# A SwiGLU and attention kernel: from slots with planned steps to one string of single-engine steps, with one ring for the three-pass blocks

## The chip, the cores and the metric

The kernel runs on one core of a Trainium2 chip. The metric is the time on the device in microseconds. Before the change it is 1538.06 us, the median of three runs (1537.92 to 1538.15). The profile is of one more execution.

The engines are TensorE (PE, with its weight loads as PEld), VectorE (DVE), ScalarE (ACT), GpSimd (POOL) and SyncE (SP), which here only issues transfers. Matrix products land in PSUM, of which the kernel uses eight banks of 128 rows by 512 fp32 numbers (five `gv`, two `acc`, one `u3`); all else lies in SBUF.

## The reference

There are four batches of 12416 rows with 128 channels. An attention with 32 inducing points squeezes each batch to 32 rows `h`, and a second one spreads `h` back over all rows. Its output goes through an RMS norm and a SwiGLU block of width 1536.

```python
def mab(q, kv):
    s = scale * (q @ kv.transpose(0, 2, 1))
    a = np.exp(s - s.max(-1, keepdims=True))
    a /= a.sum(-1, keepdims=True) + 1e-09
    return a @ kv
h = mab(I, x)                       # I: the inducing points, once per batch
x = mab(x, h).reshape(B * S, D)     # 49664 x 128

rms = np.sqrt(np.mean(x * x, axis=-1, keepdims=True) + 1e-06)
xn = x / rms * rms_g
g = xn @ w_gate                     # 128 -> 1536
val = xn @ w_val
return (g / (1 + np.exp(-g)) * val) @ w_out
```

## The kernel before

**Units and blocks.** Each batch is cut into 25 units of columns: 20 of 512, four of 480 and one of 256. The width of 1536 is cut into 12 slices `j`. A block is one slice of one unit, so there are 4 x 25 x 12 = 1200 blocks. The second attention isn't computed as such: its output is a mix of the 32 rows of `h`, so `h` is multiplied into the gate and value weights beforehand (`stack`, tiles `sg` and `sv`), and a unit enters as its attention weights, split into a high and a low half and stacked (`seam`, `gather`, tile `a`).

**One block** is made in `slot`: the gate matmul (L743), silu on ACT (L751), the value matmul (L754), and their product on DVE (L760), the factor. Gates and values share five PSUM banks (`gv`). A gate's bank is free after silu. A value's bank is free after the product, if the product goes to an SBUF tile `u`, or later, if the product stays in the bank.

**The third product**, factor times `w_out`, is summed over the 12 blocks of a unit in the bank `acc`. It has two forms. A plain block multiplies in fp32 (L676, `acc<-u,wo`). A three-pass block is split into parts that each take one pass: `hi` times one weight and `lo` times another are summed in the bank `u3` (L700, L702), and their difference `d` times a third goes to `acc` (L676). There are 819 three-pass blocks and 381 plain ones. Of the 819, 619 are "sums": the factor stays in its PSUM bank, ACT makes a scaled `hi` from it (L725) and DVE makes `lo` from `hi` and the bank (L726). The other 200 are "differences": the factor goes to SBUF, ACT makes the high half (L729), POOL makes `lo` (L730), and ACT scales the high half down (L734). In both, POOL then makes `d` in a tile of its own (L735), and afterwards all three matmuls are issued one after the other in `project3`.

**Tiles.** Three-pass blocks take sets of three SBUF tiles: four sets in old tiles of `xn`, and two more that lie in the spare `sg` and `sv` tiles and are lent for part of each batch (`lend`). Factors in SBUF take nine tiles `u0` to `u8`.

**Order.** Every engine runs its instructions in the order in which they were written. The order is made by a loop over slots. Attention and seam steps are set into slots by the lists `places`; inside a slot, the string `ordered` says where third products are issued; a split begins one slot after its product (`soon`), the difference one slot after that. A step such as `scores2` (L440) or `stack` contains the instructions of several engines. Where exponentials of the attention are near, silu is replaced by tanh, one more DVE pass (L748) and a scaled product (L757), so that ACT needn't change its table: 14 blocks.

**Other lines named below.** L448 subtracts the row maximum from the scores, both operands in SBUF: on POOL, but on DVE for the first set of a batch. L350 multiplies the maxima by a mask on DVE, both in SBUF. L279 and L287 belong to the set-up, which decodes the weights. L543 scales the attention weights on POOL, in place. L341, L390, L469, L483 and L523 are matmuls of the attention and the seams.

```python
hi, lo, d = (one[:, 0:T] for one in kws["sets"][where])
...
nc.scalar.activation(hi, v, AF.Copy, scale=(1.0 - 2.0 ** -13) * 2.0 ** -12)
nc.vector.scalar_tensor_tensor(out=lo, in0=hi.bitcast(F32), scalar=-4096.0, in1=v,
                               op0=ALU.mult, op1=ALU.add)
...
nc.gpsimd.tensor_tensor(out=d, in0=hi.bitcast(F32), in1=lo.bitcast(F32), op=ALU.subtract)
```

Of the kernel before, what the change touches and what calls it, by code (L numbers as in the profile page):

```python
# [18 lines left out]
P = 128  # L19
R = 4  # L20
# [3 lines left out]
def kernel(  # L24
# [75 lines left out]
    RING, RESERVE, HELD, SILU = 4, 7, 9, 3  # L100
    LENT = (RING, RING + 1)
# [41 lines left out]
    def load_channels(b, s, k):  # L143

        w = R * per[s]
        if not k:
            xT[b, s] = xtp.tile([P, w * m], F32, name=f"xT{s}")
        nc.sync.dma_start(out=xT[b, s][ts(k, m), :].rearrange("p (w c) -> p w c", c=m),
                          in_=xrows[ds(b * N + start[s], P * per[s]), ts(k, m)].rearrange("(i w) c -> i w c", i=m))
# [159 lines left out]
    def attention(b, load_next):  # L309
# [34 lines left out]
        def scores1(s):  # L344
            nc.vector.tensor_scalar(out=sc[b][:, cols1[s]], in0=scores(s, indT[:], R, per[s]), scalar1=1.0, scalar2=None,
                                    op0=ALU.mult, op1=ALU.max, accum_out=st["gmx"][:, s:s + 1])
# [31 lines left out]
        def sum_h(*sets):  # L378
# [12 lines left out]
            if b and sets[0]:  # L391
                nc.vector.tensor_tensor(out=hl[:, 0:C], in0=hl[:, 0:C], in1=ps[:, 0:C], op=ALU.add)
            elif b:
                nc.scalar.copy(out=hl[:, 0:C], in_=ps[:, 0:C])

        def fold_l():

            nc.vector.reduce_sum(out=st["hl"][:, C:C + 1], in_=st["ls"][:, 0:st["n"]], axis=AX.X)
            ps = bank()
            nc.tensor.matmul(ps[:, 0:1], fold[:].rearrange("p q m -> p (q m)"), st["hl"][:, C:C + 1], start=True, stop=True)  # L400
            rl = st["rl"] = small.tile([P, 1], F32, name="rl")
            nc.vector.reciprocal(out=rl[:], in_=ps[:, 0:1])
# [8 lines left out]
        def turn_h():  # L411

            ps = bank()
            nc.tensor.matmul(ps[:, 0:P], st["hn"], fold[:].rearrange("p q m -> p (q m)"), start=True, stop=True)
            hT = st["hT"] = once.tile([P, P], F32, name="hT")
            if b:
                nc.scalar.copy(out=hT[:], in_=ps[:, 0:P])
                hg = st["hg"] = once.tile([P, P], F32, name="hg")
                nc.scalar.activation(hg[:], ps[:, 0:P], AF.Copy, scale=gam)
            else:  # L420
                nc.vector.tensor_copy(out=hT[:], in_=ps[:, 0:P])
# [5 lines left out]
        def square_h():  # L427
# [4 lines left out]
            ps = bank()  # L432
            nc.tensor.matmul(ps[:, 0:m], st["hT"][:], st["hT"][:, 0:m], start=True, stop=True)
            for q in range(R):
                to, of_ = gram[b][ts(q, m), ts(q, m)], ps[ts(q, m), 0:m]
                nc.scalar.activation(to, of_, AF.Copy, bias=1e-6, scale=1.0 / C)

        def scores2(s):
            ps = scores(s, st["hT"][:, 0:m], quarters[s], per2[s])
            nc.vector.transpose(out=sc[b][rows2[s], cols2[s]], in_=ps)  # L440

        def row_max(s):
            mx = st["mx2"] = small.tile([P, 16], F32, name="mx2")[rows2[s], 0:per2[s]]
            nc.vector.reduce_max(out=mx, in_=weights(b, s), axis=AX.X)

        def sub_max(s):
            n, v, mx = per2[s], weights(b, s), st["mx2"]
# [16 lines left out]
        def stack(i):  # L464


            ps = bank()
            for c, w in enumerate(st.pop(("w", i))):
                nc.tensor.matmul(ps[ts(c, m), :], st["hg"][:, 0:m], w, start=True, stop=True)  # L469
            hi, lo = st["halves", i] = [worker([P, 512], F32R, n) for n in ("whi", "wlo")]  # L470
            rows = slice(0, NC * m)
            nc.scalar.copy(out=hi[rows, :], in_=ps[rows, :])
            nc.vector.tensor_tensor(out=lo[rows, :], in0=ps[rows, :], in1=hi[rows, :].bitcast(F32), op=ALU.subtract)
# [33 lines left out]
    def seam(b, s):  # L507
# [41 lines left out]
        def split():  # L549
# [4 lines left out]
            else:  # L554
                nc.vector.tensor_copy(out=hi[rows, 0:w], in_=aT[rows, 0:w])
            engine.tensor_tensor(out=lo[rows, 0:w], in0=aT[rows, 0:w], in1=hi[rows, 0:w].bitcast(F32), op=ALU.subtract)

        return [turn_a, square, times, scale, root, apply, turn_b, split]
# [11 lines left out]
    plain, kara, waiting = [], [], []  # L570

    def soon(k, step):

        waiting.append([k, step])

    def wait():

        for one in waiting:
            one[0] -= 1
        while any(not one[0] for one in waiting):  # L580
            one = next(one for one in waiting if not one[0])
            waiting.remove(one)
            one[1]()

    def give(group):

        for kind in group:
            (plain if kind == "p" else kara).pop(0)()

    def split_wo(step):  # L590

        if not step:
            kws["first"] = xnp.tile([P, half + NK, C], F32R, name=f"xn{full - 1}")
            rings = [xnp.tile([P, RING, 512], F32R, name=f"xn{full - 4 + n}") for n in range(3)]
            kws["sets"] = [[ring[:, n, :] for ring in rings] for n in range(RING)]
            idle.extend(range(RING))
# [10 lines left out]
        for g in range(2):  # L607
# [8 lines left out]
            if at == 4:  # L616
                nc.gpsimd.tensor_tensor(out=part(2, g)[0], in0=part(1, g)[1], in1=part(0, g)[1], op=ALU.subtract)
            if at == 6:
                scaled(0, g, 4096.0)

    idle, leaving = [], []

    def lend(b, k, idle, leaving):

        if k == (20 if not b else 2):
            idle += LENT
            return True
        if b + 1 < B and k == 184:
            leaving += [n for n in LENT if n not in idle]
            idle[:] = [n for n in idle if n not in LENT]  # L630
        assert k != 192 or not leaving

    def give_back(n, idle, leaving):

        leaving.remove(n) if n in leaving else idle.append(n)

    def lend_tiles():

        tiles = [stk.tile([P, F], F32R, name=name) for name in ("sg", "sv")]
        kws["sets"][RING:] = [[t[:, ts(n, 512)] for n in range(3)] for t in tiles]  # L640

    def split_last(step):

        n = NJ - NK
        if not step:
            kws["last"] = xtp.tile([P, 3 * n, C], F32R, name="xT0")
        one, (whi, wlo, ws) = wo[:, NK:NJ, :], (kws["last"][:, ts(kind, n), :] for kind in range(3))
        if step == 0:
            nc.scalar.activation(whi, one, AF.Copy, scale=1.0 - 2.0 ** -13)
            nc.gpsimd.tensor_tensor(out=wlo, in0=one, in1=whi.bitcast(F32), op=ALU.subtract)  # L650
        if step == 1:
            nc.scalar.activation(wlo, wlo.bitcast(F32), AF.Copy, scale=4096.0)
            nc.gpsimd.tensor_tensor(out=ws, in0=wlo.bitcast(F32), in1=whi.bitcast(F32), op=ALU.subtract)
        if step == 2:
            nc.scalar.activation(whi, whi.bitcast(F32), AF.Copy, scale=4096.0)

    def weight_of(kind, j):
        if j >= NK:
            return kws["last"][:, kind * (NJ - NK) + j - NK, :]
# [3 lines left out]
    def ffn(b, u):  # L663

        s, q = units[u]
        T = per2[s] * m
        a = moving.pop((b, u))
        sg, sv = stacks[b]
        acc = ps_acc.tile([P, 512], F32, name="acc")
        nk = sum((b, u, j) in kinds for j in range(NJ))  # L670
        st = {"left": NJ, "k": nk}
        if nk:
            st["o"] = None

        def project(lhsT, rhs, to):
            nc.tensor.matmul(to, lhsT, rhs, start=st["left"] == NJ, stop=st["left"] == 1)  # L676
            st["left"] -= 1
            if not st["left"]:
                soon(1, finish)

        def finish():
            o = st["o"] if nk else outp.tile([P, 512], F32, name="o")
            whole = o[:, 0:T].rearrange("p (q n) -> p q n", q=R)
            if nk:
                nc.vector.tensor_tensor(out=whole, in0=in_order(acc[:, 0:T]), in1=whole, op=ALU.add)
            else:
                nc.vector.tensor_copy(out=whole, in_=in_order(acc[:, 0:T]))

            def turn():
                nc.vector.transpose(out=o[:, 0:T], in_=o[:, 0:T])  # L690
                soon(2, lambda: store(o))

            soon(1, turn)

        def project3(j, where):
            if st["k"] == nk:
                st["u"] = ps_u.tile([P, 512], F32, name="u3")
            ups = st["u"]
            hi, lo, d = (one[:, 0:T] for one in kws["sets"][where])
            nc.tensor.matmul(ups[:, 0:T], weight_of(0, j), halves_in_turn(hi), start=st["k"] == nk, stop=False)  # L700
            st["k"] -= 1
            nc.tensor.matmul(ups[:, 0:T], weight_of(1, j), halves_in_turn(lo), start=False, stop=not st["k"])  # L702
            if not st["k"]:
                o = st["o"] = outp.tile([P, 512], F32, name="o")
                nc.scalar.activation(o[:, 0:T].rearrange("p (q n) -> p q n", q=R), in_order(ups[:, 0:T]), AF.Copy,  # L705
                                     scale=1.0 + 2.0 ** -12)
# [609 lines left out]
```

## Time and profile before

| | us |
|---|---|
| median of three runs | 1538.06 |
| time of the profiled execution | 1538.19 |
| span of the profiled execution, first to last instruction | 1536.4 |
| POOL differences, L735, 128 x 512: mean of one | 1.285 |
| POOL low halves, L730, 128 x 512: mean of one | 1.290 |
| DVE low halves, L726, 128 x 512: mean of one | 0.677 |
| DVE products, L760, 128 x 512: mean of one, to SBUF / in PSUM | 0.674 / 0.686 |
| ACT silu, L751, 128 x 512: mean of one | 0.600 |
| start of the first gate matmul / of the last | 47.5 / 1528.4 |

The page gives busy times by engine, the chain of waits that ended last, and groups of instructions by line. The stretch view gives busy times by engine between two moments. The timeline gives single instructions with start and length. On DVE, ACT and POOL the length of an instruction reaches a little into the next one when they follow closely: DVE instructions of 512 columns that take 0.68 start 0.60 apart, POOL's of 1.285 start 1.24 apart. All gates lie between 47.5 and 1528.4 us; before that the weights are decoded and the first batch's attention runs.

### The profile page before, as it was taken

What the parts mean: (1) busy time and instruction counts of PE and PEld (TensorE: products, weight loads), DVE (VectorE), ACT (ScalarE), POOL (GpSimd) and SP (SyncE); (2) the same over time, 40 slices, a digit from 0 to 9 for tenths busy, and PEclk for the clock granted to TensorE, in tenths of its full rate; (3) what the DMA queues carried; (4) which work ended last, traced back from release to release, by engine and by line L of the source; (5) the groups of instructions that cost most, each with busy time, mean ns of one, the idle gap of its engine ahead of it and who ended that gap; (6) DMA issues with size and microseconds to landing.
All of it is one profiled execution on the core that took longest, in us unless ns stands there. A gap on an engine that the chain in (4) does not pass through costs nothing.

```text
span 1536.4 us, 26105 instructions
## 1 busy us (share of the span) xinstructions
PE 1518.3 (99%) x7141; PEld 1091.8 (71%) x7141; DVE 1442.3 (94%) x2519; ACT 1292.2 (84%) x2501; POOL 1418.5 (92%) x1158
## 2 busy tenths in 40 slices
PE   8999999999999999999999999999999999999998
PEld 6556667767776667776777667676677777777776
DVE  6999999999999998999999999899999999999997
ACT  5777889888888889887988888978798888888886
POOL 1379999999999999999999999899989999999997
PEclk9999999999999999999999999999999999999999
DMA  7345535435453242634444323353222222122221
GB/s 282 91 81 94 97 60 114 90 78 91 67 92 69 38 93 37 137 84 86 72 78 82 56 59 77 74 120 75 49 39 39 38 36 37 34 40 38 40 40 28
DMA packets 389331, 112.58 MB, mean 73 GB/s; under 512 B 365088, under 2 KB 369728, under 8 KB 386624
## 3 DMA queue, kind: packets, MB, share of 16 engines
q1 hardware_dynamic: 388592, 110.83, 36.2%
q8 instruction: 57, 0.93, 0.3%
q14 instruction: 90, 0.74, 0.2%
q10 hardware_dynamic: 592, 0.08, 0.0%
HBM read 53.95 MB, written 27.00 MB: 53 GB/s over the span
## 4 chain that ended last, share of the span: by engine, by line
PE 90%; DVE 3%; POOL 3%; ACT 2%; issue 1%; DMA 0%; DVEq 0%; POOLq 0%; ACTq 0%
PE acc L676 30%; PE gv L743 17%; PE gv L754 16%; PE u L700 10%; PE u L702 10%; PE gv L341 3%; PE gv L523 1%; PE gv L390 1%; POOL xn L735 1%; ACT silu L751 1%; PE gv L820 1%; DVE u L760 1%; POOL xn L730 0%; DVE gv L760 0%; DMA xn<-in_x_dram 0%
## 5 line engine op out<-in xcount | busy, mean ns | idle before, releaser
L735 POOL TENSOR_TENSOR xn<-xn,xn 128x512 fp32r<-128x512 f32 (+2 forms) x626 | 767.6, 1248 | 34.1 <-DVE xn L726 11.6
L751 ACT ACTIVATE silu<-gv 128x512 f32<-128x512 f32 (+2 forms) x1186 | 683.4, 588 | 98.4 <-PE gv L743 88.1
L754 PE MATMUL gv<-a,sv 128*128 128x512 f32 (+2 forms) x1188 | 551.2, 465 | 1.0 <-ACT silu L751 0.4
L743 PE MATMUL gv<-a,sg 128*128 128x512 f32 (+2 forms) x1188 | 472.2, 398 | 1.6 <-ACT silu L751 0.6
L760 DVE TENSOR_TENSOR gv<-silu,gv 128x512 f32<-128x512 f32 (+2 forms) x616 | 410.6, 673 | 23.4 <-PE gv L754 7.5
L760 DVE TENSOR_TENSOR u<-silu,gv 128x512 f32<-128x512 f32 (+2 forms) x570 | 369.4, 655 | 24.4 <-ACT silu L751 8.8
L676 PE MATMUL acc<-u,wo 128*128 128x512 f32 (+2 forms) x762 | 371.2, 577 | 0.0
L725 ACT ACTIVATE xn<-gv 128x512 fp32r<-128x512 f32 (+2 forms) x472 | 278.1, 589 | 62.3 <-DVE gv L760 47.2
L726 DVE SCALAR_TENSOR_TENSOR xn<-xn,gv 128x512 fp32r<-128x512 f32 (+2 forms) x472 | 312.5, 662 | 13.1 <-ACT xn L725 7.4
L743 PEld LDWEIGHTS gv<-a,sg 128*128 128x128 f32 x1188 | 224.1, 189 | 137.4 <-issue 26.7
L754 PEld LDWEIGHTS gv<-a,sv 128*128 128x128 f32 x1188 | 224.3, 189 | 116.5 <-ACT silu L751 34.4
L700 PE MATMUL u<-xn,xn 128*128 128x512 f32 (+2 forms) x599 | 233.7, 390 | 0.0
L676 PE MATMUL acc<-xn,more 128*128 128x512 f32 (+2 forms) x599 | 225.7, 377 | 1.4 <-POOL xn L735 1.2
L730 POOL TENSOR_TENSOR xn<-u,xn 128x512 fp32r<-128x512 f32 (+2 forms) x154 | 191.0, 1240 | 5.1 <-ACT xn L729 4.7
L676 PEld LDWEIGHTS acc<-u,wo 128*128 128x128 f32 x762 | 142.9, 190 | 32.2 <-issue 15.4
L700 PEld LDWEIGHTS u<-xn,xn 128*128 128x128 f32 x599 | 113.3, 189 | 25.6 <-ACT o L705 8.0
L676 PEld LDWEIGHTS acc<-xn,more 128*128 128x128 f32 x599 | 113.1, 189 | 24.4 <-POOL xn L735 10.2
L735 POOL TENSOR_TENSOR sg<-sg 128x512 fp32r<-128x512 f32 (+2 forms) x97 | 123.4, 1272 | 3.6 <-DVE sg L726 1.0
L735 POOL TENSOR_TENSOR sv<-sv 128x512 fp32r<-128x512 f32 (+1 forms) x96 | 122.1, 1272 | 1.6 <-DVE xT L324 0.2
L702 PE MATMUL u<-xn,more 128*128 128x512 f32 (+2 forms) x304 | 113.0, 372 | 0.0
L702 PE MATMUL u<-xn,xn 128*128 128x512 f32 (+2 forms) x295 | 109.8, 372 | 0.0
L729 ACT ACTIVATE xn<-u 128x512 fp32r<-128x512 f32 (+2 forms) x154 | 95.3, 619 | 14.2 <-DVE u L760 9.2
(229 smaller groups left out, 1894.7 us busy)
## 6 DMA issues: line engine op xcount, KB each, us to landing
out_dram<-o SPq DMA_DIRECT2D x320, 64.0 KB, 2.0
xT<-in_x_dram SPq DMA_DIRECT2D x60, 256.0 KB, 3.9
xn<-in_x_dram SPq DMA_DIRECT2D x60, 256.0 KB, 5.0
a<-hi SPq DMA_DIRECT2D x156, 64.0 KB, 2.0
a<-lo SPq DMA_DIRECT2D x156, 64.0 KB, 2.0
xn<-in_x_dram SPq DMA_DIRECT2D x5, 1024.0 KB, 9.7
xn<-w SPq DMA_DIRECT2D x18, 256.0 KB, 3.0
out_dram<-o SPq DMA_DIRECT2D x64, 60.0 KB, 2.0
```

What stands on the lines that cost most here:

```text
L676: nc.tensor.matmul(to, lhsT, rhs, start=st["left"] == NJ, stop=st["left"] == 1)
L700: nc.tensor.matmul(ups[:, 0:T], weight_of(0, j), halves_in_turn(hi), start=st["k"] == nk, stop=False)
L702: nc.tensor.matmul(ups[:, 0:T], weight_of(1, j), halves_in_turn(lo), start=False, stop=not st["k"])
L725: nc.scalar.activation(hi, v, AF.Copy, scale=(1.0 - 2.0 ** -13) * 2.0 ** -12)
L726: nc.vector.scalar_tensor_tensor(out=lo, in0=hi.bitcast(F32), scalar=-4096.0, in1=v, op0=ALU.mult, op1=ALU.add)
L729: nc.scalar.activation(d, v, AF.Copy, scale=1.0 - 2.0 ** -13)
L730: nc.gpsimd.tensor_tensor(out=lo, in0=v, in1=d.bitcast(F32), op=ALU.subtract)
L735: nc.gpsimd.tensor_tensor(out=d, in0=hi.bitcast(F32), in1=lo.bitcast(F32), op=ALU.subtract)
L743: nc.tensor.matmul(g[:, 0:T], sg[:, ts(j, P)], halves_in_turn(a[:, 0:T]), start=True, stop=True)
L751: nc.scalar.activation(sl[:, 0:T], g[:, 0:T], AF.Silu)
L754: nc.tensor.matmul(v[:, 0:T], sv[:, ts(j, P)], halves_in_turn(a[:, 0:T]), start=True, stop=True)
L760: nc.vector.tensor_tensor(out=t[:, 0:T], in0=sl[:, 0:T], in1=v[:, 0:T], op=ALU.mult)
```

## The change

The loop over slots goes. After the first 26 blocks, which keep their form, one string of about 10,500 letters gives the whole order: each letter is one step of one engine, and a dot stands for the next attention or seam step from a list of numbers. Steps that held several engines' instructions are cut into single-engine ones. The sort of each block is a letter too: P plain, S, T or D. S is as "sums" was. D is as "differences" was. T is new: its factor goes to an SBUF tile `u` as for D, and its halves are made as for S, by ACT and DVE. There are 476 S, 178 T, 166 D and 380 P; 28 blocks use tanh.

All three-pass blocks now take two tiles, `hi` and `lo`, from one ring of 19 tiles that plain factors use as well: the nine `u` tiles and ten in the old `xn` tiles. `sg` and `sv` are lent no more. The first two matmuls are issued on their own (`project_two`); then POOL adds `hi` to `lo` in place of `lo`, and the third matmul reads that. Signs are turned so that it is a sum.

```diff
-    RING, RESERVE, HELD, SILU = 4, 7, 9, 3
-    LENT = (RING, RING + 1)
+    RING, HELD, SILU = 4, 9, 3
...
-            kws["sets"] = [[ring[:, n, :] for ring in rings] for n in range(RING)]
+            kws["room"] = [ring[:, ts(n, 512)] for ring in rings for n in range(RING)][:3 * RING - 2]
...
         def scores1(s):
-            nc.vector.tensor_scalar(out=sc[b][:, cols1[s]], in0=scores(s, indT[:], R, per[s]), ...)
+            st["s1", s] = scores(s, indT[:], R, per[s])
+
+        def evict1(s):
+            nc.vector.tensor_scalar(out=sc[b][:, cols1[s]], in0=st.pop(("s1", s)), ...)
...
+    def times_value():
+        n, b, u, j = next_of("m")
+        one, kind = unit_of(b, u), kinds[n]
+        T, v, sl = one["T"], values.pop(n), silus.pop(n)
+        if kind in "Ss":
+            factor_of[n] = {"u": v[:, 0:T]}
+        else:
+            factor_of[n] = {"u": factor()[:, 0:T]}
...
+    def high():
...
+        hi = t["hi"] = room()[:, 0:T]
+        t["lo"] = room()[:, 0:T]
+        if kind in "Dd":
+            nc.scalar.activation(hi, t["u"], AF.Copy, scale=1.0 - 2.0 ** -13)
+        else:
+            nc.scalar.activation(hi, t["u"], AF.Copy, scale=-(1.0 - 2.0 ** -13) * 2.0 ** -12)
...
+    def low():
+        n = lists["l"].pop(0)
+        t = factor_of[n]
+        nc.vector.scalar_tensor_tensor(out=t["lo"], in0=t["hi"].bitcast(F32), scalar=4096.0, in1=t["u"],
+                                       op0=ALU.mult, op1=ALU.add)
...
+    def low_of_u():
+        nc.gpsimd.tensor_tensor(out=t["lo"], in0=t["u"], in1=t["hi"].bitcast(F32), op=ALU.subtract)
+    def high_down():
+        nc.scalar.activation(t["hi"], t["hi"].bitcast(F32), AF.Copy, scale=-(2.0 ** -12))
+    def project_two():
+        nc.tensor.matmul(ups, weight_of(0, j), halves_in_turn(t["hi"]), start=not one["q"], stop=False)
+        nc.tensor.matmul(ups, weight_of(1, j), halves_in_turn(t["lo"]), start=False, stop=last)
+    def add_in_place():
+        nc.gpsimd.tensor_tensor(out=t["lo"], in0=t["hi"].bitcast(F32), in1=t["lo"].bitcast(F32), op=ALU.add)
+    def project_third(name):
+        project(n, weight_of(2, blocks[n][2]), halves_in_turn(factor_of[n]["lo"]), False)
...
+    for name in "".join(program.split()):
+        if name == ".":
+            step, args = micros[int(next(taken))]
+            step(*args)
+        else:
+            do[name]()
```

## The prediction

> **What bounds the kernel now.** I read the busy totals first, then the stretches, then single instructions on the timeline.
>
> ```profile
> span 1536.4 us, 26105 instructions
> PE 1518.3 (99%) x7141; PEld 1091.8 (71%) x7141; DVE 1442.3 (94%) x2519; ACT 1292.2 (84%) x2501; POOL 1418.5 (92%) x1158
> PE 90%; DVE 3%; POOL 3%; ACT 2%; issue 1%; DMA 0%; DVEq 0%; POOLq 0%; ACTq 0%
> 0.00:50.00 50.00, 43.09 (x464) 31.69 (x464) 35.78 (x103) 28.31 (x61) 9.95 (x20) 1.00 0.61 230
> 50.00:100.00 50.00, 48.22 (x173) 25.23 (x174) 46.65 (x77) 36.36 (x62) 24.04 (x22) 1.00 0.51 99
> 450.00:500.00 50.00, 50.00 (x208) 34.97 (x207) 49.43 (x85) 43.88 (x85) 49.45 (x40) 1.00 0.42 73
> 1500.00:1536.00 36.00, 31.57 (x155) 25.38 (x153) 28.74 (x57) 24.50 (x55) 28.73 (x28) 1.00 0.19 29
> ```
>
> In a stretch line the columns are length, then busy PE, weight loads, DVE, ACT, POOL, then clock and DMA. The reader should see three engines near full at once: PE ends the chain 90% of the time, but in a good stretch DVE (49.43 of 50) and POOL (49.45) have nothing to spare either. ACT has room, and the DMA rows end almost nothing.
>
> PE's 99% hides stalls, because a matmul's modelled length (0.38 us) is longer than its step. Consecutive steps start 0.215 apart:
>
> ```profile
> 700.07 0.38 PE L754 MATMUL gv<-a,sv 128*128 128x512 f32 x1
> 700.28 0.38 PE L743 MATMUL gv<-a,sg 128*128 128x512 f32 x1
> 700.50 0.38 PE L700 MATMUL u<-xn,xn 128*128 128x512 f32 x1
> ```
>
> The FFN has 5094 passes of 512 columns (a plain block counts four), 1028 of 480 and 259 of 256. By 0.215, 0.202 and 0.110 us that is 1095 + 208 + 28 = 1331. The attention's matmul lines (L341, L390, L523, L469, L483) were busy 102 us between 47.5 and 1528, overlapped ends included; I take 77. So PE needs about 1408 of the 1481 us between first and last gate: some 70 us of stall is all that a better order can win.
>
> **The change, part by part.** *PE:* counted in the changed program, 5104, 1020 and 256 passes: 1097 + 206 + 28 = 1331 again. The clock column is 1.00 throughout. Worth 0.
>
> *POOL:* before, 819 differences (L735) and 200 low halves (L730); after, 820 additions in place and 166 low halves: 31 fewer at 512 columns and 2 fewer at 256, by 1.24 us from start to start, -40 us. No row has an in-place add of two full operands. The in-place rows with one broadcast operand (L448, L543) cost 1.05, L735 costs 1.285. I take 1.285, the nearest; the lower end would give back another 190, on an engine that then isn't the bound.
>
> *ACT:* 33 fewer scalings, -16 us on an engine at 84%: 0 on the path. The smaller steps carry the same attention instructions, and SP issues the same 1079 transfers. The gathers and loads keep their counts and DMA lies under PE; 0, though a late gather would stall all twelve gates of a unit (about 14 us).
>
> *DVE:* low halves made by DVE go from 504, 96 and 19 (512, 480, 256 columns) to 515, 112 and 27; tanh blocks from 14 to 28, each with one more DVE pass. At 0.60, 0.57 and 0.35 from start to start: 6.6 + 9.1 + 2.8 + 8.4 = +27 us, on an engine that is full.
>
> *The new order:* counted along PE's order, a gate now stands 1.72 us ahead of its value instead of 0.87, and the fifth-percentile distance to the next tenant of a bank rises from 3.02 to 3.45 us for a value held until its low half is made. That is looser. The third matmul now stands 3.7 us (median) behind the pair that it must follow, and the addition between costs 1.29, so that this new PE-POOL-PE trip is covered. Its gain lies between 0 and the 70 us of stall; alone I would take 25.
>
> *The new sort of block, T.* 178 blocks make the low half on DVE from a factor kept in SBUF, not in PSUM. `low` then reads `hi` and `u`, both in SBUF. None of the 619 old low halves did: theirs was one SBUF and one PSUM operand (L726, 0.677). The trace of before has the same kind of read in L448, L350 and the set-up's L279, and it shows what happens when POOL is at work:
>
> ```profile
> 320.55 1.16 DVE L448 TENSOR_TENSOR sc<-sc,mx 128x512 f32<-128x512 f32 x1
> 321.12 1.73 POOL L730 TENSOR_TENSOR xn<-u,xn 128x512 fp32r<-128x512 f32 x1
> 49.52 1.31 DVE L279 SCALAR_TENSOR_TENSOR we<-sv,we 128x512 int32<-128x512 int32 x1
> 49.02 1.26 POOL L287 TENSOR_TENSOR xn<-o,we 128x512 f32<-128x512 f32 x1 [4.90 <-PE gv L743]
> 699.63 0.67 DVE L448 TENSOR_TENSOR sc<-sc,mx 128x512 f32<-128x512 f32 x1
> 699.84 1.61 POOL L735 TENSOR_TENSOR xn<-xn,xn 128x512 fp32r<-128x512 f32 x1 [0.85 <-DVE xn L726]
> ```
>
> At 320.55 POOL was inside an operation that ended 0.61 later: L448 took 1.16 instead of 0.67 and ended 0.55 after it. At 49.52 the POOL operation ended 0.76 later: L279, the very instruction of `low`, took 1.31 instead of its usual 0.68. When DVE came first, at 699.63, POOL's operation took 1.61 instead of 1.28. The extra is thus what is left of POOL's operation less 0.12. If a T low comes at any moment of a 1.285 us operation, the mean is 1.165 x 1.165 / 2 / 1.285 = 0.53. POOL would be busy about nine tenths of the time: 0.48 each, 178 x 0.48 = 85 us on DVE. The bounds are 0 (each falls into a POOL gap) and 178 x 1.07 = 190 (two of L350's three rows waited a whole operation, 1.24 and 1.26 against 0.18). I take 85, since POOL's queue, not DVE's phase, decides, and the changed order leaves no room for it: the next DVE step stands 0.57 us of PE work behind a T low, 0.64 behind a PSUM one. POOL's next operation loses 0.45 (1.73 against 1.28) in nine of ten cases, +72 us. Behind the waiting low on DVE stand products of silu and value, which free PE's banks, so that PE waits next.
>
> The Trainium skill, SBUF - State Buffer (section Who interferes with whom), says that a VectorE instruction with two SBUF inputs contends with a GpSimd instruction that reads SBUF, and that the later one waits for the whole of the other; it says this against T. Taken to the letter the wait is all that remains, 0.64 on average, so 178 x 0.9 x 0.64 = 103 us, and the sum below would end near 1586 instead.
>
> **The sum.** DVE: 1442.3 + 27 + 85 = 1554. On the trace 243 of its instructions stood behind a gap of 0.1 us or more, and each of these shows 0.68 where its neighbours follow each other in 0.60; with DVE full they close up, -19: 1535. The idle that stays: 14.2 and 3.4 in the first two stretches (the opening is nearly unchanged), 7.3 in the last, and 0.57 of 50, the loss of the fullest stretch, over 1400 us of flow, 16. Total 1576. Not every T low costs on the path where DVE would have waited anyway (69 us of idle between 100 and 1500 before, about a tenth of it hit): -8. **1568 us**. POOL: 1418.5 - 40 + 72 = 1450, plus 66 idle in the opening and 7 at the end, 1523: below DVE. PE: 1536.4 - 70 = 1466: below both. The profiled run took 1538.2 with a span of 1536.4; the median is 1538.06, so 2 us more than the span lies under my rounding. Within 0.2% (3 us) of the median is what a measurement of this kernel can't tell from no change.
>
> **The rivals.**
> (B) *The waits vanish and the looser order wins.* For it: a PE stall of 70 us, POOL 40 us lighter, and banks freed early by T. Then DVE is 1442 + 27 - 19 = 1450, with 25 idle at the ends and 2% of the flow (28): 1503; half of PE's stall remaining gives 1501. I put it at 1508. It decides when a T low costs less than about 0.14 us on average: (1535 - 1510) / 178. Against: in five of the six rows of L448 and L350 one of the two engines waits for the other.
> (C) *Two full engines block each other.* POOL's loss delays additions, third matmuls and the ring's tiles, and the idle of DVE grows from 1.1% to 4% of the flow: +40, so 1608.
> (D) *It doesn't do what it says:* the loosened order and the waits cancel, 1536 to 1541.
>
> **How the numbers follow.** My forecast (1540 to 1600) 0.66, B 0.22, C 0.08, D 0.04. Slower 0.66 + 0.08 = 0.74, same 0.04, faster 0.22. The likeliest's own range is 1540 to 1600. The unknown costs alone would make it 1503 to over 1608; to leave out no more than 2 in 10 I reach into B and C: 1508 to 1606.
>
> **What would show it.** The rows of `low` with an SBUF factor near 1.16 us against 0.68 from PSUM; the POOL additions' mean up from 1.285 towards 1.36 (64 us over 820); DVE busy above 1520 and more than 48.5 of 50 through the flow; PE's weight loads waiting on DVE more than now. If the two forms of `low` cost the same, step T is wrong and B has it. If additions in place cost clearly under or over 1.285, POOL's step is wrong. If the third matmuls wait on POOL for more than some 20 us, the covered trip was not covered.

## The result, and the profile after

| | us |
|---|---|
| before, median of four runs beside it (1537.92 to 1538.15) | 1538.09 |
| changed kernel, median of four runs (1622.56 to 1633.92) | 1628.89 |
| ratio, with its 95% interval | 1.0588 (1.0546 to 1.0631) |
| predicted, with its range | 1568 (1508 to 1606) |

The change made the kernel 5.9% slower. The direction was right. The size was not: 91 us were lost where 30 were forecast, and the time lies 23 us above the range.

The page of the changed kernel, busy totals and the chain of work that ended last:

```profile
span 1630.3 us, 25701 instructions
PE 1552.7 (95%) x7142; PEld 1091.1 (67%) x7142; DVE 1567.9 (96%) x2568; ACT 1280.3 (79%) x2468; POOL 1431.7 (88%) x1125
PE 69%; DVE 15%; issue 6%; POOL 6%; ACT 3%; DMA 1%; SPq 0%; DVEq 0%; POOLq 0%; ACTq 0%
```

PE ended the chain for 90% of the span before, now for 69%; DVE went from 3% to 15%, and its busy time from 1442.3 to 1567.9 us. The stretch view (length, then busy PE, weight loads, DVE, ACT, POOL, then clock, DMA share and GB/s) shows it over the whole flow, 1500 us long:

```profile
100.00:1600.00 1500.00, 1435.46 (x6380) 1011.28 (x6379) 1463.97 (x2344) 1198.37 (x2302) 1373.89 (x1061) 0.99 0.33 63
```

DVE is busy 97.6% of it, 48.8 of every 50 us. The view of one source line gives the shortest, median and longest of each form in ns. For L743, the low halves on DVE, the two forms with `gv` are S blocks, with one operand in PSUM; the two that end in `u` are T blocks, with both operands in SBUF:

```profile
L743 DVE SCALAR_TENSOR_TENSOR xn<-xn,gv x249: 374/672/689, 103.6 to 1622.0; 128x512 fp32r<-128x512 f32 x96, 128x480 fp32r<-128x480 f32 x25, 128x256 fp32r<-128x256 f32 x4
L743 DVE SCALAR_TENSOR_TENSOR u<-xn,gv x227: 397/673/689, 150.4 to 1621.3; 128x512 fp32r<-128x512 f32 x87, 128x480 fp32r<-128x480 f32 x21, 128x256 fp32r<-128x256 f32 x6
L743 DVE SCALAR_TENSOR_TENSOR u<-xn,u x95: 440/1152/5485, 138.9 to 1506.9; 128x512 fp32r<-128x512 f32 x75, 128x480 fp32r<-128x480 f32 x15, 128x256 fp32r<-128x256 f32 x5
L743 DVE SCALAR_TENSOR_TENSOR xn<-xn,u x82: 552/1168/5808, 106.1 to 1523.7; 128x512 fp32r<-128x512 f32 x72, 128x480 fp32r<-128x480 f32 x7, 128x256 fp32r<-128x256 f32 x3
```

None of the 476 S lows took longer than 0.689 us. The T lows have a median of 1.16, and the longest took 5.81. Together the 178 T lows (one more stands in a form of its own) took 235.5 us. At the 0.66 us that a T low takes with POOL idle (sixth experiment) it would be 117.5: the waits cost DVE 118 us. The timeline shows what the longest waited for, first DVE, then POOL (start, length, both in us; x2 stands for two of a kind in a row):

```profile
901.29 0.70 DVE L724 TENSOR_TENSOR gv<-silu,gv 128x512 f32<-128x512 f32 x1
901.89 5.81 DVE L743 SCALAR_TENSOR_TENSOR xn<-xn,u 128x512 fp32r<-128x512 f32 x1
907.62 0.68 DVE L724 TENSOR_TENSOR u<-silu,gv 128x512 f32<-128x512 f32 x1
...
900.98 1.28 POOL L580 TENSOR_TENSOR lo<-aT,hi 128x512 fp32r<-128x512 f32 x1
902.21 2.50 POOL L789 TENSOR_TENSOR u<-xn,u 128x512 fp32r<-128x512 f32 x2
904.67 2.48 POOL L789 TENSOR_TENSOR xn<-xn,xn 128x512 fp32r<-128x512 f32 x2
```

The low began inside a POOL operation that ended at 902.26. It did not get its turn then. Four more POOL operations followed each other without a gap, none of them longer than usual, and the low ended 0.55 after the last of them (907.15). Eleven of the 178 were passed over like this; they lasted 2.5 to 5.8 us, 48.6 together. The other 167 took 186.9 us, 1.12 each.

What waited behind them is seen in the view of the waits (waiter, what it waited for, us in total, times, longest):

```profile
ACT silu L692 <- PE gv L682: 144.7, 234, 4.2
PEld gv L682 <- DVE u L724: 42.4, 81, 4.9
POOL u L789 <- PE u L770: 41.3, 32, 3.4
```

PE's weight loads wait up to 4.9 us for DVE (before: at most 1.0), because a product of silu and value that stands behind a T low frees a bank late. ACT then waits for PE's gates, 145 us against 88, and POOL for PE's pairs. The loss goes round through all four engines.

One thing that the text ahead of the prediction says too widely: the 19 tiles are one ring by numbering, but the string uses six of them (`u0` to `u5`) for factors alone and the other 13 for halves alone.

### The profile page after: what moved, and what is told of

It is laid out like the page before. It is cut to its first block, busy times and chain, and to the rows that moved or that the text cites. A ratio compares the mean times of both kernels' runs of the same rounds, so it can differ in the third digit from the quotient of the medians.

```text
span 1630.3 us, 25701 instructions
## 1 busy us (share of the span) xinstructions
PE 1552.7 (95%) x7142; PEld 1091.1 (67%) x7142; DVE 1567.9 (96%) x2568; ACT 1280.3 (79%) x2468; POOL 1431.7 (88%) x1125
## 4 chain that ended last, share of the span: by engine, by line
PE 69%; DVE 15%; issue 6%; POOL 6%; ACT 3%; DMA 1%; SPq 0%; DVEq 0%; POOLq 0%; ACTq 0%
PE acc L781 23%; PE gv L682 13%; PE gv L710 12%; PE u L770 8%; PE u L769 8%; DVE u L724 4%; DVE u L743 3%; DVE xn L743 3%; POOL xn L789 2%; POOL u L789 2%; PE gv L340 2%; DVE gv L724 2%; ACT silu L692 1%; PE gv L392 1%; PE gv L544 1%
## 5 line engine op out<-in xcount | busy, mean ns | idle before, releaser
L692 ACT ACTIVATE silu<-gv 128x512 f32<-128x512 f32 (+2 forms) x1172 | 667.3, 587 | 198.7 <-PE gv L682 144.7
L789 POOL TENSOR_TENSOR u<-xn,u 128x512 fp32r<-128x512 f32 (+2 forms) x403 | 513.1, 1287 | 53.4 <-PE u L770 40.9
L789 POOL TENSOR_TENSOR xn<-xn,xn 128x512 fp32r<-128x512 f32 (+2 forms) x343 | 449.4, 1322 | 36.5 <-PE u L770 25.4
L724 DVE TENSOR_TENSOR u<-silu,gv 128x512 f32<-128x512 f32 (+2 forms) x704 | 451.6, 655 | 20.1 <-PE gv L710 8.1
L724 DVE TENSOR_TENSOR gv<-silu,gv 128x512 f32<-128x512 f32 (+2 forms) x468 | 305.0, 666 | 6.5 <-PE gv L710 3.9
L743 DVE SCALAR_TENSOR_TENSOR xn<-xn,gv 128x512 fp32r<-128x512 f32 (+2 forms) x249 | 162.1, 657 | 2.8 <-ACT xn L737 2.2
L743 DVE SCALAR_TENSOR_TENSOR u<-xn,gv 128x512 fp32r<-128x512 f32 (+2 forms) x227 | 147.7, 656 | 3.6 <-ACT xn L737 2.8
L781 PE MATMUL acc<-u,more 128*128 128x512 f32 (+2 forms) x330 | 144.9, 440 | 1.3 <-POOL u L789 1.2
L743 DVE SCALAR_TENSOR_TENSOR u<-xn,u 128x512 fp32r<-128x512 f32 (+2 forms) x95 | 128.4, 1354 | 1.3 <-ACT xn L737 1.0
L737 ACT ACTIVATE xn<-u 128x512 fp32r<-128x512 f32 (+2 forms) x177 | 109.3, 620 | 20.4 <-DVE u L724 17.5
L734 ACT ACTIVATE xn<-u 128x512 fp32r<-128x512 f32 (+2 forms) x163 | 101.2, 622 | 26.9 <-DVE u L724 24.1
L750 POOL TENSOR_TENSOR u<-u,xn 128x512 fp32r<-128x512 f32 (+2 forms) x81 | 105.9, 1309 | 15.0 <-ACT xn L734 8.5
```

The costliest lines, as they stand in the source:

```text
L692: nc.scalar.activation(sl[:, 0:T], gates.pop(n)[:, 0:T], AF.Silu)
L724: nc.vector.tensor_tensor(out=to, in0=sl[:, 0:T], in1=v[:, 0:T], op=ALU.mult)
L734: nc.scalar.activation(hi, t["u"], AF.Copy, scale=1.0 - 2.0 ** -13)
L737: nc.scalar.activation(hi, t["u"], AF.Copy, scale=-(1.0 - 2.0 ** -13) * 2.0 ** -12)
L743: nc.vector.scalar_tensor_tensor(out=t["lo"], in0=t["hi"].bitcast(F32), scalar=4096.0, in1=t["u"], op0=ALU.mult, op1=ALU.add)
L750: nc.gpsimd.tensor_tensor(out=t["lo"], in0=t["u"], in1=t["hi"].bitcast(F32), op=ALU.subtract)
```

## The experiments

Theory L: the reads of two SBUF operands, which wait for POOL, are the whole loss. Rivals: O, the new order, the ring or the additions in place cost the time; R, such a read is dear in itself, whatever POOL does.

**1. T lows with one operand.** In T blocks `low` reads only `hi`, so `u` is left out of the low half.

```diff
+        if kinds[n] == "T":
+            nc.vector.tensor_scalar(out=t["lo"], in0=t["hi"].bitcast(F32), scalar1=4096.0, scalar2=None,
+                                    op0=ALU.mult, op1=ALU.max, accum_out=ones)
+        else:
             nc.vector.scalar_tensor_tensor(out=t["lo"], in0=t["hi"].bitcast(F32), scalar=4096.0, in1=t["u"], ...)
```

> The changed kernel, but the low half of all 178 T blocks is made from hi alone (a scaled copy that also writes out its running maximum): one SBUF operand in place of two; u is left out of it. All else, order and tiles, is as changed. Theory L (DVE and POOL shut each other out where a DVE instruction reads two SBUF operands): these lows fall from a mean of 1.32 us to about 0.68 (+0.08 for the maximum's own read), DVE busy from 1568 to about 1466, POOL's additions back to 1.28, and the time to 1500 to 1525 us, under the kernel before. Rival O (the order, the ring of two tiles and the addition in place that the third matmul waits for are what costs): at least 1600 us. Rival M (both, about half each): 1550 to 1590.

Measured: 1515.56 us (1515.26 to 1516.82), 0.985 of before (0.9835 to 0.9865). The totals:

```profile
PE 1496.7 (99%) x7142; PEld 1092.9 (72%) x7142; DVE 1454.1 (96%) x2746; ACT 1270.2 (84%) x2468; POOL 1370.2 (91%) x1125
```

T's largest form in the view of its line:

```profile
L744 DVE TENSOR_SCALAR_CACHE_REDUCE u<-xn x95: 404/679/691, 133.5 to 1392.3; 128x512 fp32r<-128x512 f32 x75, 128x480 fp32r<-128x480 f32 x15, 128x256 fp32r<-128x256 f32 x5
```

The largest of POOL's additions among the groups of instructions (count, busy us, mean ns, idle before):

```profile
L793 POOL TENSOR_TENSOR u<-xn,u 128x512 fp32r<-128x512 f32 x319 | 404.5, 1282 | 25.7 <-PE u L774 20.2 <-DVE gv L724 2.1 <-DVE u L722 1.5
```

With the same order, ring and additions, the time falls by 113 us, to 23 below the kernel before. No T row is longer than 0.691. POOL's additions go from 1.327 back to 1.282, the price of the old differences (1.285): adding in place costs nothing extra. O falls. PE is full again.

**2. Every second T block so.** 89 T lows keep two operands; the rest is as in the first.

```diff
-        if kinds[n] == "T":
+        ts_seen.append(n) if kinds[n] == "T" else None
+        if kinds[n] == "T" and len(ts_seen) % 2:
```

> As the run with one operand for all T blocks, but for every second one (89 of 178; u is left out of those). Theory L with a price per instruction: half way between that run and the changed kernel, about 1565 to 1575 us. If DVE has room to take half of the waits: within 20 us of the run with all of them. Rival O: at least 1600 us.

Measured: 1596.17 (1587.96 to 1601.34), ratio 1.0367 (1.0331 to 1.0404). A miss: not half of the loss came back but under a third. The 89 lows left:

```profile
L749 DVE SCALAR_TENSOR_TENSOR u<-xn,u x47: 446/1255/4856, 134.3 to 1475.6; 128x512 fp32r<-128x512 f32 x34, 128x480 fp32r<-128x480 f32 x9, 128x256 fp32r<-128x256 f32 x4
L749 DVE SCALAR_TENSOR_TENSOR xn<-xn,u x41: 674/1228/5922, 120.9 to 1491.2; 128x512 fp32r<-128x512 f32 x38, 128x480 fp32r<-128x480 f32 x3
```

They summed to 138.8 us, 80 more than unblocked: 0.90 each, against 0.66 (118 / 178) in the changed kernel. The time again lies above the first experiment by about the sum of the waits: 1596.2 - 1515.6 = 81. Twelve of the 89 were passed over for more than 2.5 us. So the price isn't a fixed sum for each low; a minority of very long waits makes a large part of it.

**3. The same read in the kernel before.** 178 of its 619 low halves read `wo`, in SBUF, in place of the factor in the bank; these halves are not those of the reference.

```diff
-                nc.vector.scalar_tensor_tensor(out=lo, in0=hi.bitcast(F32), scalar=-4096.0, in1=v, ...)
+                two = len(sums_seen) * 178 // 619 > (len(sums_seen) - 1) * 178 // 619
+                nc.vector.scalar_tensor_tensor(out=lo, in0=hi.bitcast(F32), scalar=-4096.0,
+                                               in1=wo.rearrange("p j c -> p (j c)")[:, 0:T] if two else v, ...)
```

> The kernel before, but 178 of its 619 DVE low halves, spread evenly, read a part of the output weights (SBUF) in place of the factor in its PSUM bank; the factor is left out of those. Nothing else changes. Theory L: these lows take 1.2 to 1.4 us, DVE busy goes from 1442 to about 1555, POOL's mean rises by about 0.07, the time to 1595 to 1640 us. Rival O: nothing but noise, 1535 to 1545 us.

Measured: 1624.0 (1623.69 to 1624.31), ratio 1.0553 (1.0536 to 1.0571). The two largest forms of that line:

```profile
L729 DVE SCALAR_TENSOR_TENSOR xn<-xn,gv x339: 407/675/690, 87.9 to 1607.2; 128x512 fp32r<-128x512 f32 x134, 128x480 fp32r<-128x480 f32 x31, 128x256 fp32r<-128x256 f32 x5
L729 DVE SCALAR_TENSOR_TENSOR xn<-xn,wo x133: 419/1258/3411, 110.5 to 1611.4; 128x512 fp32r<-128x512 f32 x104, 128x480 fp32r<-128x480 f32 x23, 128x256 fp32r<-128x256 f32 x6
```

The one operand alone gives the kernel before nearly the whole loss, 86 us, with the old order, the old tiles and no addition in place. The 178 lows summed to 216.2, 98 more than unblocked. Only three were passed over here.

**4. All T blocks plain.** Nothing is left out here: each T block becomes a plain one (sort t, in a list of its own), one more pass of PE each, and no `low` reads two SBUF operands.

```diff
-        lists["p" if kind == "P" else "h"].append(n)
+        lists["p" if kind == "P" else "t" if kind == "t" else "h"].append(n)
...
+          "t": lambda: project_plain("t"), ...
```

> The changed kernel with all T blocks made plain: their factor stays in its SBUF tile and is multiplied in fp32 where the first pair of matmuls stood; scaling, low half, addition and third pass fall away for them. Seven tiles hold factors and twelve hold halves. PE gains 178 passes of 0.215, +38 us, and DVE loses 178 instructions, POOL and ACT as many. Theory L: 1505 to 1535 us, PE alone being the bound. Rival O: at least 1590 us, since order, ring and addition in place stay for the other 642.

Measured: 1553.01 (1552.69 to 1556.63), ratio 1.0097 (1.0082 to 1.0112), a miss.

```profile
PE 1534.5 (99%) x6964; PEld 1066.2 (69%) x6964; DVE 1371.7 (88%) x2390; ACT 1198.3 (77%) x2290; POOL 1162.9 (75%) x947
```

PE is full, the others are far from it. 178 passes of 0.2155 us are 38 us, and 1515.6 + 38 = 1554: the added passes come on top of the first experiment in full. My expectation had let PE's stalls absorb some of them.

**5. A searched string with 10 T left.** The strings of steps, sorts, banks and tiles are replaced, with the step t of the fourth. T blocks become S, D or plain, and some others change their sort too (513 plain in all). The first row of the sorts, for the others look alike:

```diff
-        DPDPSTPPPSDPPTPPTDSPTDDTTDTPSTPPPDDDSDPDSPDPTTPPSSPSPPDDPPPDTPSDPSSSSDPPSSDPDDSSSPSPPSSPSTSSPPSPDSDPSSTPTSPTTD
+        DDDPttPPPSDPPDPPtDSPTDtDSDDPtSPPPDtDDtPDSPtPSSPPDDPSPPDtPPPDSPtDPSSDSSPPSSDPDDSSSPSPPSSDtSSDPPSPDSDPSStPSSPtSD
```

> The changed kernel with another string, in which only 10 of the 178 blocks of sort T are left: 392 S, 285 D, 10 T, 513 plain (133 more plain than before, so 133 passes of PE more than the changed kernel, 133 x 0.2155 = 29 us), the ring and the additions in place kept. Its output is the reference's. Theory L (the two-operand reads wait for POOL, and nothing else in the change costs time): DVE loses only about 10 x 0.9 = 9 us to waits, no engine but PE is full, and the time lies at 1505 to 1530, below the kernel before. Rival O (the new order, the ring or the additions in place cost the time): 1600 or more. Rival N (order is worth nothing here and PE's added passes come on top of the 1515.6 of the first experiment): 1515.6 + 29 = 1544, slower than before.

Measured: 1595.99 (1595.77 to 1596.19), ratio 1.0371 (1.0357 to 1.0385). A miss by 66 us, and it would have fitted O, were it not for the first experiment. DVE is busy only 85%. The timeline of ACT shows one reason:

```profile
208.03 0.58 ACT L689 ACTIVATE silu<-gv 128x512 f32<-128x512 f32 x1
208.63 1.28 ACT L692 ACT_TABLE_LOAD   x1
209.92 0.60 ACT L692 ACTIVATE silu<-gv 128x512 f32<-128x512 f32 x1
210.42 0.59 ACT L737 ACTIVATE xn<-gv 128x512 fp32r<-128x512 f32 x1
211.03 1.28 ACT L371 ACT_TABLE_LOAD   x1
```

My string mixes the attention's exponentials (L371) with silu (L692; L689 is the tanh in its place), and between the two ACT loads a function table, 1.28 us. There are 32 such loads here (the expectation of the seventh experiment says 31), 16 before and after the change; a load of rows also came 4 us late for PE. How much of the 66 us each of these made is not shown. The ten T lows took 12.5 us together and none was passed over, so this says little on T. It says that an order with few T can be slow for its own reasons. (The string has 391 S and 286 D, one off from the expectation.)

**6. No additions on POOL.** The 820 additions in place are left out, the third matmul reads `lo`; T lows keep both operands.

```diff
-        nc.gpsimd.tensor_tensor(out=t["lo"], in0=t["hi"].bitcast(F32), in1=t["lo"].bitcast(F32), op=ALU.add)
         lists["r"].append(n)
```

> The changed kernel without POOL's 820 additions in place (the third matmul then reads lo, so the output is another); all 178 T lows keep their two SBUF operands. POOL's busy time falls from 1432 to about 500 us, a third of the span. Theory L (a T low waits for what is left of POOL's operation): it is hit in about one case of three, so the 178 lows sum to about 118 + 178 x 0.33 x 0.6 = 153 us instead of 235, none waits over 2.5 us, and the time is 1490 to 1525. Rival R (the read of two SBUF operands is dear in itself, whatever POOL does): the lows still sum to over 220 us, DVE stays full and the time is 1590 or more.

Measured: 1517.99 (1517.9 to 1518.43), ratio 0.9864 (0.9851 to 0.9878). The totals:

```profile
PE 1497.7 (99%) x7142; PEld 1095.0 (72%) x7142; DVE 1459.8 (96%) x2568; ACT 1270.1 (84%) x2468; POOL 392.0 (26%) x305
```

T's two forms in the view of the line:

```profile
L743 DVE SCALAR_TENSOR_TENSOR u<-xn,u x95: 403/681/1655, 134.1 to 1395.3; 128x512 fp32r<-128x512 f32 x75, 128x480 fp32r<-128x480 f32 x15, 128x256 fp32r<-128x256 f32 x5
L743 DVE SCALAR_TENSOR_TENSOR xn<-xn,u x82: 418/680/1767, 104.8 to 1410.4; 128x512 fp32r<-128x512 f32 x72, 128x480 fp32r<-128x480 f32 x7, 128x256 fp32r<-128x256 f32 x3
```

The same instruction with the same two operands takes 0.68 (median) when POOL is mostly idle, 26% busy. The 178 sum to 128.4 us; the 129 that met no POOL operation took 0.660 on average. R falls. Taking away either side of the meeting, DVE's second operand (first experiment) or POOL's work (this one), gives the same time within 2.5 us.

**7 to 10. Other strings without T.** These leave nothing out either; again only the strings differ. In the seventh the table loads are kept at 16 and the loads of rows get more room; 11 T are left. The eighth is the seventh with these 11 made plain; the other steps keep their order, and only the numbers of banks and tiles are dealt out anew. The ninth and tenth have no T, and more slack at each hand-over. The same row of the seventh and the eighth:

```diff
-        tDtPDDPPPtDPPtDPTDSDttDtDttSDtPSPDtDDDPDSPDPttPPDSPDPPDDPPPSDPtDPSStDDPPSSDPDDSDSPSPPSSPSDSSPPSPtDDPSSDPtSPSDD
+        tDtPDDPPPtDPPtDPtDSDttDtDttSDtPSPDtDDDPDSPDPttPPDSPDPPDDPPPSDPtDPSStDDPPSSDPDDSDSPSPPSSPSDSSPPSPtDDPSSDPtSPSDD
```

> A second string with 11 T left: 399 S, 295 D, 11 T, 495 plain (115 more plain than the changed kernel, 115 passes x 0.2155 = 25 us of PE). Unlike the string of the fifth experiment it keeps 16 loads of ACT's function table (that one had 31, at 1.28 us each, against 16 before and after the change) and leaves more room ahead of the loads of rows. Its output is the reference's. Theory L (T's waits were the change's whole loss, and the fifth experiment was slow through its table loads and late rows): 1512 to 1550, DVE under 90%, PE at 98% or more, no lock waits. If the fifth experiment was slow for another reason that also holds here (D's and plain blocks in place of T cost what T cost): 1580 or more.

Measured: 1557.03 (1555.75 to 1559.28), ratio 1.0126 (1.0109 to 1.0143), 7 us above the expectation. Two of the eleven T lows left were passed over, one of them here, DVE first, then PE:

```profile
647.24 4.93 DVE L743 SCALAR_TENSOR_TENSOR xn<-xn,u 128x512 fp32r<-128x512 f32 x1
652.10 0.15 DVE L410 RECIPROCAL rl<-gv 128x1 f32<-128x1 f32 x1
...
648.86 0.78 PE L710 MATMUL gv<-a,sv 128*128 128x512 f32 x1
652.31 0.48 PE L710 MATMUL gv<-a,sv 128*128 128x512 f32 x1 [2.67 <-DVE rl L410]
```

PE then stood still for 2.67 us, until DVE had emptied a bank. In that stretch, 600 to 700, the granted clock was 0.97.

> The string of the seventh experiment with its last 11 T blocks made plain (506 plain, 11 more passes of PE, 2.4 us), nothing else. Two of those 11 lows were passed over there (5.15 and 4.93 us at 608.9 and 647.2, where PE then stalled and its granted clock fell to 0.97), and all 11 sum to 19.5 us against some 7 unblocked. Theory L: the stalls behind them go, 5 to 15 us less than the 1557.0 there: 1542 to 1552. Rival (DVE was only 87% busy, so waits there are covered): 1557 to 1562, by the added passes.

Measured: 1547.33 (1546.81 to 1547.94), ratio 1.0062 (1.0046 to 1.0077), 9.7 us less in spite of 11 more passes. Eleven T lows had cost 12 us (9.7 + 2.4), as much as their waits (19.5 - 7.5 = 12), although DVE was busy only 87%: spare time on DVE didn't cover these waits. The mean granted clock was 0.996 in the seventh and 1.000 in the eighth; what the lower clock added isn't separated.

> A third string without any T: 378 S, 309 D, 513 plain (133 more plain than the changed kernel, 133 x 0.2155 = 29 us of PE), 16 table loads, chosen so that each hand-over between engines has some 0.1 us more of slack than in the seventh experiment. Its output is the reference's. Theory L (with no T and an order with slack, what remains is PE's own work): 1515 to 1545; below 1535 it beats both kernels. If added plain passes come in full on top of the first experiment: 1515.6 + 28.7 = 1544. If orders without T are slow for another reason: 1555 or more.

> A fourth string without any T: 393 S, 300 D, 507 plain (127 more plain, 27 us of PE), 16 table loads, hand-overs with less slack than in the ninth experiment but more than in the seventh. Its output is the reference's. Theory L: 1515 to 1545, within some 8 us of the ninth experiment; if slack decides, it lies between that one and the eighth.

Measured: 1540.23 (1539.7 to 1542.39), ratio 1.0015 (1.0006 to 1.0023), and 1539.22 (1538.88 to 1541.08), ratio 1.001 (1.0002 to 1.0019). The totals of the tenth:

```profile
PE 1519.0 (99%) x7015; PEld 1086.9 (71%) x7015; DVE 1335.2 (87%) x2307; ACT 1278.8 (83%) x2475; POOL 1381.0 (90%) x1132
```

They beat the changed kernel by 89 and 90 us, and neither beats the kernel before. The tenth has less slack than the ninth and is no slower, so slack did not decide between them. 133 and 127 added plain blocks at 0.2155 on the 1515.6 of the first experiment give 1544 and 1543: what the better order gains, the plain blocks that replace T give back. Of the versions that leave nothing out, none tried was faster than the kernel before.

## Why the prediction was right or wrong

**PE, worth 0.** Right. The work was unchanged, and with T's waits gone PE is full again (99% in the first and sixth). But the clock was not 1.00 throughout: the granted clock of the changed kernel was 0.97 or 0.98 in six of the fifteen stretches of 100 us between 100 and 1600, and 0.992 in the mean. The loss doesn't need this, since the third experiment lost 86 us at a clock of 0.999; how much the lower clock added in the changed kernel is not shown.

**POOL, additions in place at 1.285.** Right: 1.282 to 1.284 without T's waits.

**The new order, "alone I would take 25".** Right: 1538.1 - 1515.6 = 23 in the first, 20 in the sixth. These hold the rest of the change too, all but T's waits (and in the sixth POOL's additions).

**The mechanism of T.** Right, as the first, third and sixth experiments show. Of the 178 T lows 164 began inside a POOL operation, and the median of length less what was left of that operation was 0.550 us, as in the row at 320.55. The rule of the Trainium skill (SBUF — State Buffer, section Who interferes with whom) says that the later one waits for the whole of the other, and these rows agree. The eleven that waited for several operations go beyond that rule; there the measurement decides.

**The size of T's wait, 85 us.** This is the first step that failed: DVE lost 118. The 167 that were not passed over cost 187 - 167 x 0.66 = 77 us, 0.46 each against the 0.48 taken. The eleven that were cost 48.6 - 11 x 0.66 = 41, where the formula gives 11 x 0.48 = 5. My formula let a low wait for one POOL operation at most; the bound of 190 would have held this, but I took the mean of a wait that ends with one operation. The trace of before had no such case among the six rows of L448 and L350.

**POOL's loss, +72.** Too large: 986 additions and low halves took 1287.7 us against 1232.9 in the first experiment, 55. The operations that pass a low over take no longer than usual (rows at 902.21 and 904.67), so POOL loses nothing there.

**Idle DVE, 14.2 + 3.4 + 7.3 + 16 = 41.** The second step that failed: 1630.3 - 1567.9 = 62. The ends held, 26 against 25. The flow did not: between 100 and 1600 us DVE was idle for 36 of 1500, 2.4%, and I had taken 1.1%, the loss of the fullest stretch of 50 us, for all of it. T's waits did not make this idle time. The first experiment, without them, has 35 of 1400 (DVE's busy time is the 1364.74 in this line of its stretch view):

```profile
100.00:1500.00 1400.00, 1395.92 (x6454) 1027.50 (x6453) 1364.74 (x2549) 1201.38 (x2332) 1328.98 (x1075) 1.00 0.35 67
```

Rival C let POOL's loss raise the idle share to 4%. That did not come; its 1608 lies nearer to the result than my 1568, but not for its reason.

**The -8 for waits that were covered anyway.** Wrong. From the first experiment to the changed kernel DVE's waits rose by 118 and the time by 113, and DVE's idle time did not shrink (1513.4 - 1454.1 = 59, then 62): little or nothing was covered. The eighth shows the same where DVE is 87% busy.

**The sum.** DVE's busy time was forecast as 1554 less 19: with 118 for 85 it is 1568, and the trace has 1567.9. The terms without T held: 1442.3 + 27 - 19 = 1450, and the sixth has 1459.8 with 11 us of waits in it, 1449 without. With 62 idle 1568 is the span, 1630. From the forecast to the span: 1568 + 33 (T's waits) + 21 (idle) + 8 (covered waits) = 1630. The profiled execution took 1632.0; the four runs range over 11 us, so the balance holds to within some microseconds only.

**The signs named beforehand.** T lows at 1.16 against 0.68: met. POOL's additions from 1.285 towards 1.36: 1.327 and 1.361 in the two largest groups. DVE above 1520 and over 48.5 of 50: met, 1567.9 and 48.8. PE's weight loads waiting on DVE: met. The third matmuls' weight loads did wait 47 us for POOL's additions, above the 20 named, but none over 0.8 us, and PE itself stood still behind them for under 3: that trip was covered after all, and the sign was badly chosen.

**Rivals.** B (1508) is what the kernel does once the waits are gone: 1515.6. D is excluded by the interval.

## What to carry to other kernels

Before a factor is moved from PSUM to SBUF to free a bank, look whether an instruction on VectorE then reads two SBUF operands while GpSimd is busy; such an instruction is priced by GpSimd's queue, not by its own length. Price it with its tail, not its mean: a few waits of several operations made a third of the loss, and they stop every engine behind them even where VectorE has time to spare. And when a step's price is removed in an experiment by other work, price that work as fully as the step: here the plain blocks that replaced T cost what the better order had won.

## What the runs showed of the hardware that I had not expected

A VectorE instruction that waits for GpSimd need not be next when GpSimd's operation ends. It was passed over by up to four further operations that followed without a gap: 11 of 178 in the changed kernel, 12 of 89 in the second experiment, 2 of 11 in the seventh, 3 of 178 in the third. I found nothing in the traces (offset within the operation, kind of the next one, semaphores) that tells these cases from those that got their turn; this stays open.

A `tensor_scalar` on DVE with one SBUF operand and an accumulator took 0.679 and a read of the accumulator 0.084 more, and it waited for no POOL operation (the first experiment, with POOL 91% busy).
